# Decode attention with conditioned layer norms: one section of w_mod loaded later, in eight transfers of eight partitions

## The chip, the core and the metric

One core of a Trainium2 chip runs the whole program. It has TensorE (PE, with its weight loads listed apart as PEld), VectorE (DVE), ScalarE (ACT), GpSimd (POOL) and SyncE (SP), which here only issues transfers, and 16 DMA engines that move data from HBM into the 128 partitions of SBUF. The metric is the device time of one execution in microseconds.

## What is computed

One token is decoded for each of 4 batch rows. x and c are 4 x 512; the K and V caches have 32 heads, 4096 positions and 128 numbers a head, in bf16, 128 MB each. Everything else is small beside them.

```python
    x = A_x
    mod = (_silu(c) @ w_mod).reshape(c.shape[0], 6, 1, -1)
    sa, ca, ga, sb, cb, gb = (mod[:, 0].copy(), mod[:, 1].copy(), mod[:, 2].copy(), mod[:, 3].copy(), mod[:, 4].copy(), mod[:, 5].copy())
    h = _layernorm(x, axis=-1) * (1 + ca) + sa
    x = x + ga * _A_ref(h, A_k_cache, A_v_cache, A_wq, A_wo)
    h = _layernorm(x, axis=-1) * (1 + cb) + sb
    x = x + gb * _B_ref(h, B_w_in, B_w_sp, B_b_sp, B_w_out)
    return x
```

_A_ref is softmax attention over the caches with wq before it and wo behind it. _B_ref is a gated MLP: gelu(x @ w_in) is split in two halves of 896, the second is normalised and gates the first, and w_out brings it back to 512. w_mod is 512 x 3072, so each of its six sections (sa, ca, ga, sb, cb, gb) is 512 x 512, 0.5 MB.

## The kernel before

The caches are cut into 32 tiles (NT) of 4 heads of one batch row. A tile of K, and one of V, is 4 MB: each partition gets 32 KB that lie together in HBM. Iteration i of the main loop works on tile i in stages that are spread over iterations: `mult` (L288, DVE) multiplies K by the query in two halves, `reduce_d` (L294, PE) sums over the 128 numbers with an identity matmul, `sum8` and `scores` (L303 to L326, DVE and ACT) make the maximum and the exponentials of tile i - 1, `pv` (L366, PE) multiplies tile i - 2 by V, and `o_pick`, `o_cols` and `o_scale` (L374 to L408) finish tile i - 3.

The order of all instructions is written out by hand, and each engine takes its own in that order. All large loads are issued by SP, one queue, in program order: wq_sb (L89), wm_sb (L92), K of tiles 0 and 1 and V of tile 0 (L104), and then, in iteration i, K of tile i + 2 and V of tile i. K tiles have two buffers named "kt", V tiles two named "vt". A K load waits until both `mult` and `reduce_d` of the buffer's old tile are done; a V load waits for `pv` of its old tile. A wait of SP holds up every transfer behind it.

What the change touches:

- wm_sb (L90 to L92) holds the first five sections of w_mod: row p*4 + j lies in partition p. `mod_cols` (L236 to L245) multiplies chosen sections by cT, the transposed silu(c): sections 0 and 1 ahead of the loop (L254), sections 2, 3 and 4 in iteration 2 (L571 to L573), whose result is modT. Section 5 is loaded at the end into a "vt" buffer (wg_sb, L600 to L602) and used at L715.
- c (c_sb) and x (x_sb) are loaded by ACT (L83, L85), four rows each. `rows_to_cols` (L184) transposes them on PE; the silu runs on the transposed c, 128 x 16 (L224 to L234).
- cbT, the part of modT for section 4, gets 1 added in iteration 5 (L593). It is used at L645 and L658.
- After iteration 2 the pool with wq_sb and wm_sb is given back, and the pool wts takes its place: wo_sb, wo_last, win_sb and wout_sb.
- In iteration 30 the last loads are queued: V of tile 31 in five pieces into a "kt" buffer, win_sb (L597), wout_sb (L599), wg_sb (L602).
- Behind the loop the last tiles are finished, and then come the MLP's matmuls, `gate` (L684) on win_sb, L707 on wout_sb, L715 on wg_sb, and the output (L753).

Of the kernel before, what the change touches and what calls it, by code (L numbers as in the profile page):

```python
# [8 lines left out]
BF16 = mybir.dt.bfloat16  # L9
F32 = mybir.dt.float32  # L10
AF = mybir.ActivationFunctionType
ALU = mybir.AluOpType
# [12 lines left out]
def kernel(  # L25
# [16 lines left out]
    nc = tc.nc  # L42
    P = 128
    B, _, D = A_x.shape
    _, H, SK, DH = A_k_cache.shape
    F = B_w_in.shape[1]
    FH = F // 2
    DJ = D // P
    NF = F // P
    NH = FH // P  # L50
    NJ = SK * HQ // P
# [13 lines left out]
    consts = ctx.enter_context(tc.tile_pool(name="consts", bufs=1))  # L65
    kvp = ctx.enter_context(tc.tile_pool(name="kv", bufs=2))
# [6 lines left out]
    def ps_sm(shape, dtype=F32):  # L73
        return psum.tile(shape, dtype, name="sm", bufs=3)
# [6 lines left out]
    pre = pre_cm.__enter__()  # L81
    c_sb = pre.tile([B, D], BF16, name="c_sb")
# [4 lines left out]

    wq_sb = pre.tile([P, DJ, H * DH], BF16, name="wq_sb")
    nc.sync.dma_start(out=wq_sb, in_=A_wq.rearrange("(p j) n -> p j n", p=P))  # L89
    wm_sb = pre.tile([P, DJ, 5 * D], BF16, name="wm_sb")  # L90
    wm = w_mod.rearrange("(p j) n -> p j n", p=P)
    nc.sync.dma_start(out=wm_sb, in_=wm[:, :, 0:5 * D])  # L92

    def kv_view(cache, i):
        g, b = divmod(i, B)
# [16 lines left out]
    def load_v(i):  # L112
# [8 lines left out]
    ident_bf = consts.tile([P, P], BF16, name="ident_bf")  # L121
# [13 lines left out]

    st2 = consts.tile([P, 2, DJ + 1], F32, name="st2")
    nc.vector.memset(st2, 0.0)
    nc.vector.memset(st2[:, 1, DJ:], LN_EPS * D / P)

# [3 lines left out]
        out=sel32, in_=ident_f.rearrange("p (q r) -> p r q", r=R), axis=AX.X, op=ALU.add  # L143
# [10 lines left out]
    for g in range(G):  # L154
        nc.vector.tensor_reduce(out=selg[:, g:g + 1], in_=idr[:, g], axis=AX.XY, op=ALU.add)
    nc.vector.tensor_reduce(
        out=sel4, in_=ident_f.rearrange("p (c b) -> p b c", b=B), axis=AX.X, op=ALU.add
# [3 lines left out]
        out=mask8, in_=ident_f.rearrange("p (h u) -> p h u", h=2 * HQ), axis=AX.X, op=ALU.add  # L161
# [3 lines left out]
    x1w = consts.tile([P, DJ, R], F32, name="x1w")  # L165
    nc.gpsimd.memset(x1w, 0.0)
    cT = consts.tile([P, DJ, B], BF16, name="cT")

    consts.tile([P, 512], mybir.dt.uint8, name="gap")
    wk.tile([P, 32], mybir.dt.uint8, name="gap", bufs=1)  # L170
    pbds, opss = [], []
    for k in range(3):
        t = consts.tile([P, NJ, HQ], BF16, name=f"pbd{k}")
        nc.gpsimd.memset(t, 0.0)
        pbds.append(t)
    for k in range(2):
        t = psum.tile([P, G, DH], F32, name=f"ops{k}", bufs=1)
# [3 lines left out]
    def bc(ap, n):  # L181
        return ap[:, None, :].to_broadcast([P, n, ap.shape[-1]])

    def rows_to_cols(src):  # L184
        t = ps_sm([P, DJ, B], BF16)
        for j in range(DJ):
            nc.tensor.transpose(t[:, j, :], src[0:B, j:D:DJ], ident_bf[0:B, 0:B])
        return t

    def across(rhs, mat):  # L190
# [13 lines left out]
    def normed(pool, src, name, then=None, last=None):  # L204
# [16 lines left out]
        rsqrt(rs, v, 1.0, eps)  # L221
        return xc, rs

    cps = rows_to_cols(c_sb)  # L224
    cx = pre.tile([P, DJ, B], F32, name="cx")
    nc.vector.tensor_copy(out=cx, in_=cps)
    sg = pre.tile([P, DJ, B], F32, name="sg")
    nc.vector.tensor_scalar(
        out=sg, in0=cx, scalar1=-60.0, scalar2=-1.0, op0=ALU.max, op1=ALU.mult
    )  # L230
    nc.scalar.activation(out=sg, in_=sg, func=AF.Exp)
    nc.vector.tensor_scalar_add(out=sg, in0=sg, scalar1=1.0)
    nc.vector.reciprocal(out=sg, in_=sg)
    nc.vector.tensor_tensor(out=cT, in0=cx, in1=sg, op=ALU.mult)  # L234

    def mod_cols(s0, n, dst):  # L236

        for m in range(n):
            s, j = divmod(m, DJ)
            c0 = (s0 + s) * D + j  # L240
            for k in range(DJ):
                nc.tensor.matmul(  # L242
                    dst[:, m, :], lhsT=wm_sb[:, k, c0:c0 + (P - 1) * DJ + 1:DJ], rhs=cT[:, k, :],
                    start=(k == 0), stop=(k == DJ - 1),
                )  # L245
# [11 lines left out]
        out=hs, in0=modA[:, DJ:2 * DJ, :], scalar=1.0, in1=xn, op0=ALU.add, op1=ALU.mult  # L257
# [174 lines left out]
    for n in set(SETS):  # L432
        picks[n] = consts.tile([P, n, P], BF16, name=f"pick{n}")
        for a in range(n):
            u = P // n
            nc.vector.tensor_copy(
                out=picks[n][:, :, a * u:(a + 1) * u],
                in_=ident_bf.rearrange("p (u r) -> p r u", r=n),
# [77 lines left out]
        nc.vector.tensor_tensor(out=a, in0=a, in1=wp, op=ALU.add)  # L516

    modT = consts.tile([P, 3 * DJ, B], F32, name="modT")

    g8 = consts.tile([P, 2, B], F32, name="g8")  # L520
    sp_t = consts.tile([1, 2], BF16, name="sp_t")
# [8 lines left out]
    for i in range(NT):  # L530
        more = list(QPLAN.get(i, ()))
        mult(i, 0)
        if i >= 1:
            scores(i - 1)
        if i >= 2:
            norm_b(i - 2)
        add_up()
        rows_up()
        dealt()
        if i >= 3:  # L540
            o_pick(i - 3)
        reduce_d(i, 0)
        if i >= 3:
            o_cols(i - 3)
        if more:
            queries(more.pop(0))
        mult(i, 1)
        if i >= 1:
            norm_r(i - 1)
        if i >= 3:  # L550
            o_scale(i - 3)
        sum8(i, 0)
        reduce_d(i, 1)
        load_k(i + 2)
        if i >= 1:
            norm_a(i - 1)
        project()
        if i - 3 in ends:
            deal(ends[i - 3])
        while more:  # L560
            queries(more.pop(0))
        if i >= 2:
            pv(i - 2)
        if i == 0:
            load_v(1)
        elif 2 <= i < L:
            load_v(i)
        if i == 2:
            nc.scalar.dma_start(out=sp_t[:, 0:1], in_=B_w_sp[0:1, 0:1])
            nc.scalar.dma_start(out=sp_t[:, 1:2], in_=B_b_sp.rearrange("(a b) -> a b", b=1))  # L570
            mps = ps_sm([P, 3 * DJ, B])  # L571
            mod_cols(2, 3 * DJ, mps)
            nc.vector.tensor_copy(out=modT, in_=mps)  # L573
            pre_cm.__exit__(None, None, None)
            wts = tl = ctx.enter_context(tc.tile_pool(name="wts", bufs=1))
            wo_sb = wts.tile([P, H - HQ, D], BF16, name="wo_sb")
            wo_last = wts.tile([P, HQ, D], BF16, name="wo_last")
            hl = (H - HQ) * DH
            h0 = 0
            for n in SETS:  # L580
                nc.sync.dma_start(
                    out=wo_sb[:, h0:h0 + n, :],
                    in_=A_wo[h0 * DH:(h0 + n) * DH].rearrange("(p r) n -> p r n", p=P),
                )
                h0 += n
            nc.sync.dma_start(out=wo_last, in_=A_wo[hl:H * DH].rearrange("(q p) n -> p q n", p=P))
        if i == 5:
            sps = ps_sm([P, 2])
            nc.tensor.matmul(sps, lhsT=ones_b, rhs=sp_t, start=True, stop=True)
            nc.vector.tensor_copy(out=spf, in_=sps)  # L590
            nc.vector.tensor_copy(out=g8[:, 1, :], in_=spf[:, 0:1].to_broadcast([P, B]))
            cbT = modT[:, 2 * DJ:3 * DJ, :]
            nc.vector.tensor_scalar_add(out=cbT, in0=cbT, scalar1=1.0)  # L593
        if i == L - 1:
            load_v(L)
            win_sb = wts.tile([P, DJ, F], BF16, name="win_sb")
            nc.sync.dma_start(out=win_sb, in_=B_w_in.rearrange("(p j) n -> p j n", p=P))  # L597
            wout_sb = wts.tile([P, NH, D], BF16, name="wout_sb")
            nc.sync.dma_start(out=wout_sb, in_=B_w_out.rearrange("(j p) n -> p j n", p=P))  # L599
            wg_sb = kvp.tile([P, NJ, DH], BF16, name="vt", bufs=2)  # L600
            wg_sb = wg_sb.rearrange("p n d -> p (n d)")[:, 0:DJ * D].rearrange("p (k n) -> p k n", k=DJ)
            nc.sync.dma_start(out=wg_sb, in_=wm[:, :, 5 * D:])  # L602

    gaT = modT[:, 0:DJ, :]
# [24 lines left out]
    def sums():  # L629
# [21 lines left out]
        out=nv2, in0=mq2[:, 0:1], scalar=mq2[:, 0:1], in1=mq2[:, 1:2],  # L651
        op0=ALU.mult, op1=ALU.subtract,
# [6 lines left out]
        out=hl, in0=xs, scalar=mq2[:, 0:1], in1=cbT[:, :, BL], op0=ALU.subtract, op1=ALU.mult  # L659
    )  # L660
    nc.vector.scalar_tensor_tensor(
        out=hT2[:, :, BL], in0=hl, scalar=rsl, in1=sbT[:, :, BL], op0=ALU.mult, op1=ALU.add
# [4 lines left out]
        out=x1m, in0=x1[:, :, :, None].to_broadcast([P, DJ, B, HQ]),  # L667
        in1=mask4[:, None, None, :].to_broadcast([P, DJ, B, HQ]), op=ALU.mult,
    )
    x1r = ps_sm([B * DJ, P])  # L670
    for k in range(DJ):
        nc.tensor.matmul(
            x1r[:, k:P:DJ], lhsT=x1m[:, k].rearrange("p b j -> p (b j)"), rhs=sel32,
            start=True, stop=True,
# [4 lines left out]
    def gate(h):  # L679
# [21 lines left out]
        out=zz.rearrange("p f g b -> p g b f"), in0=z1[:, None].to_broadcast([P, 2, B, NH]),  # L701
        in1=st3[:, 0:2], op=ALU.mult,
    )
    y = ps_q()[:, 0:DJ * 2 * B].rearrange("p (j g b) -> p j g b", j=DJ, g=2)
    for j in range(DJ):
        for f in range(NH):
            nc.tensor.matmul(  # L707
                y[:, j], lhsT=wout_sb[:, f, j * P:(j + 1) * P], rhs=zz[:, f],
                start=(f == 0), stop=(f == NH - 1),
# [3 lines left out]
    for j in range(DJ):  # L713
        for k in range(DJ):
            nc.tensor.matmul(  # L715
                gb[:, j, :], lhsT=wg_sb[:, k, j * P:(j + 1) * P], rhs=cT[:, k, :],
                start=(k == 0), stop=(k == DJ - 1),
# [3 lines left out]
        out=mq3, in_=ps3.rearrange("p (g b f) -> p g b f", g=2, b=B), axis=AX.X, op=ALU.add  # L721
# [4 lines left out]
        out=rs3, in0=mq3[:, 1], scalar=LN_EPS, in1=rs3, op0=ALU.add, op1=ALU.subtract  # L726
# [3 lines left out]
        out=g8[:, 0, :], in0=mq3[:, 0, :], scalar=-1.0, in1=g8[:, 1, :], op0=ALU.mult, op1=ALU.mult  # L730
# [5 lines left out]
        out=t3[:, 2], in0=yb[:, 0], scalar1=spf[:, 1:2], scalar2=None, op0=ALU.mult  # L736
    )
    nc.vector.tensor_tensor(
        out=g8, in0=g8, in1=rs3[:, None, :].to_broadcast([P, 2, B]), op=ALU.mult
    )  # L740
    nc.vector.tensor_tensor(
        out=t3[:, 0:2], in0=g8[:, :, :, None].to_broadcast([P, 2, B, DJ]), in1=yb, op=ALU.mult
# [3 lines left out]
        out=tt, in_=t3.rearrange("p g b j -> p b j g"), axis=AX.X, op=ALU.add  # L746
# [37 lines left out]
```

## Time and profile before

| what | value |
|---|---|
| time, median of 3 runs | 667.87 us (667.51 to 667.99) |
| span of the profiled execution | 665.8 us |
| bytes read from HBM | 282.73 MB, 425 GB/s over the span |
| PE, DVE, ACT busy | 60%, 63%, 13% |
| DMA share of 16 engines, 20 to 620 us | 1.00, at 432 GB/s |
| a K load, from issue to landing (31 of them) | 23.0 us, median |
| a V load, from issue to landing (31 of them) | 30.7 us, median |
| granted TensorE clock, mean | 0.828 |

The span is from the first instruction to the last on the profiled core; the runs' times include what lies around it, some 2 us. Slices and groups of the page are means over the whole execution; the end of the kernel is read from the chain of waits and the timeline. A queue "instruction" in the DMA table moves the program itself, not data. The trace also lists each DMA packet with its start, length, size and queue; it does not name the engine.

### The profile page before, as it was taken

Reading aid. Unit: us, or ns where it says so; the run is one execution under the profiler, and the core shown is the slowest. Engines: PE = TensorE matmul, PEld = TensorE weight load, DVE = VectorE, ACT = ScalarE, POOL = GpSimd, SP = SyncE. Lnnn points to the kernel's source line nnn. Section 1 sums busy time; section 2 is a strip of 40 time slices with the busy share of each in tenths; the row PEclk is TensorE's granted clock in tenths of the full one; section 3 lists DMA queues with packets and bytes.
Section 4 is the critical chain, followed back from the end, with each engine's and each line's share of the span. In section 5 each row is a group of like instructions: output and inputs, shape, how many; then the busy total and the mean of one; then the engine's idle time right before and its main releaser. Section 6 shows DMA issues by size and latency. Waiting matters only on the chain.

```text
span 665.8 us, 6509 instructions
## 1 busy us (share of the span) xinstructions
PE 399.3 (60%) x2674; PEld 175.4 (26%) x2674; DVE 419.5 (63%) x589; ACT 85.0 (13%) x278; POOL 3.8 (1%) x17
## 2 busy tenths in 40 slices
PE   1195795556556746754665467566555468666675
PEld 0132331222222312222222222222222223322245
DVE  3485592776565777655567756657765566776833
ACT  1021120111011111101111110111111011111112
POOL 1000000000000000000000000000000000000000
PEclk9998987777898778789877778787777897887975
DMA  8999999999999999999999999999999999999996
GB/s 363 452 419 433 431 417 435 436 437 422 439 432 438 422 439 433 436 423 436 435 431 426 438 435 432 426 436 437 431 426 437 435 429 432 433 436 421 438 419 234
DMA packets 13377, 283.15 MB, mean 425 GB/s; under 512 B 1308, under 2 KB 3236, under 8 KB 4132
## 3 DMA queue, kind: packets, MB, share of 16 engines
q1 hardware_dynamic: 13328, 282.73, 98.9%
q8 instruction: 21, 0.34, 0.2%
q14 instruction: 8, 0.07, 0.0%
q10 hardware_dynamic: 20, 0.01, 0.0%
HBM read 282.73 MB, written 0.00 MB: 425 GB/s over the span
## 4 chain that ended last, share of the span: by engine, by line
DMA 56%; DVE 28%; PE 13%; issue 1%; SPq 1%; ACT 0%; DVEq 0%
DMA kt<-in_A_k_cache_dram 52%; DVE kt L288 21%; PE red L294 11%; DMA win_sb<-in_B_w_in_dram 5%; DVE osb L378 2%; DVE S L303 1%; DVE mrow L312 1%; DVE osb L374 1%; PE ops L366 1%; SPq L104 1%; DVE mt L316 1%; DVE nM L318 0%; PE qps L274 0%; DVE mb L314 0%; DVE nM L319 0%
## 5 line engine op out<-in xcount | busy, mean ns | idle before, releaser
L294 PE MATMUL red<-kt,ident_bf 128*128 128x512 bf16 x1024 | 301.5, 461 | 236.4 <-DVE kt L288 236.4
L288 DVE TENSOR_TENSOR kt<-kt,qbc 128x8192 bf16<-128x8192 bf16 x64 | 282.8, 4420 | 185.2 <-DMA kt<-in_A_k_cache_dram 184.2
L294 PEld LDWEIGHTS <-ident_bf 128*128 128x128 bf16 x1024 | 118.9, 116 | 411.5 <-issue 285.8
L326 ACT ACTIVATE pbd<-S,nM 32x128 bf16<-32x128 f32 x128 | 73.8, 577 | 505.3 <-DVE nM L319 463.2
L366 PE MATMUL ops<-vt,pbd 128*16 128x512 bf16 x992 | 62.6, 388 | 1.4 <-DMA vt<-in_A_v_cache_dram 1.4
L303 DVE TENSOR_REDUCE S<-red 128x64 f32<-128x512 f32 x64 | 43.8, 684 | 5.8 <-PE red L294 5.8
L378 DVE SCALAR_TENSOR_TENSOR osb<-ops,selg,osb 128x128 f32<-128x128 f32 x93 | 32.6, 351 | 3.3
L326 ACT ACTIVATION_READ_ACCUMULATOR pbd<-S,nM 32x1 f32 x128 | 32.0, 250 | 0.0
L366 PEld LDWEIGHTS <-pbd 128*16 128x16 bf16 x992 | 23.2, 90 | 30.7 <-issue 8.5
L386 PEld LDWEIGHTS sm<-sel,osb 128*128 128x128 f32 x62 | 11.7, 194 | 7.4 <-issue 2.2
L374 DVE TENSOR_SCALAR osb<-ops,selg 128x128 f32<-128x128 f32 x31 | 10.1, 325 | 5.3 <-PE ops L366 5.3
L386 PE MATMUL sm<-sel,osb 128*128 128x4 f32 x62 | 9.2, 219 | 2.1 <-DVE osb L378 2.0
L278 ACT CAST qbc<-qps 128x512 bf16<-128x512 f32 x8 | 4.7, 585 | 45.3 <-PE qps L274 45.3
L274 PE MATMUL qps<-wq_sb,hTb 128*32 128x512 bf16 x128 | 9.2, 412 | 1.6 <-DVE hTb L262 0.9
L312 DVE TENSOR_REDUCE mrow<-S 128x1 f32<-128x128 f32 x32 | 9.2, 286 | 1.1
L242 PE MATMUL sm<-cT,wm_sb 128*128 128x4 bf16 x80 | 3.0, 173 | 8.3 <-DMA wm_sb<-in_w_mod_dram 8.3
L316 DVE STREAM_TRANSPOSE mt<-mb 128x32 f32<-128x32 f32 x32 | 6.8, 212 | 1.1
L337 DVE TENSOR_SCALAR rsb<-mask,rs 128x4 f32<-128x4 f32 x32 | 7.2, 224 | 0.4 <-ACT pbd L326 0.4
L318 DVE TENSOR_REDUCE nM<-mt 128x1 f32<-128x32 f32 x32 | 6.0, 186 | 1.1
L314 DVE COPY mb<-mrow 128x32 f32<-128x32 f32 x32 | 5.8, 181 | 1.1
L491 PE MATMUL sm<-wo_sb,od 128*4 128x512 bf16 x24 | 5.7, 379 | 0.0
L319 DVE TENSOR_SCALAR nM<-nM 128x1 f32<-128x1 f32 x32 | 4.9, 153 | 1.1
(136 smaller groups left out, 88.8 us busy)
## 6 DMA issues: line engine op xcount, KB each, us to landing
kt<-in_A_k_cache_dram SPq DMA_DIRECT2D x31, 4096.0 KB, 23.0
vt<-in_A_v_cache_dram SPq DMA_DIRECT2D x31, 4096.0 KB, 30.7
wq_sb<-in_A_wq_dram SPq DMA_DIRECT2D x1, 4096.0 KB, 12.3
kt<-in_A_k_cache_dram SPq DMA_DIRECT2D x2, 2048.0 KB, 16.7
wo_sb<-in_A_wo_dram SPq DMA_DIRECT2D x3, 1024.0 KB, 22.9
kt<-in_A_v_cache_dram SPq DMA_DIRECT2D x3, 1024.0 KB, 25.5
wm_sb<-in_w_mod_dram SPq DMA_DIRECT2D x1, 2560.0 KB
win_sb<-in_B_w_in_dram SPq DMA_DIRECT2D x1, 1792.0 KB
```

The costliest lines, as they stand in the source:

```text
L274: nc.tensor.matmul(qp[R * q:R * (q + 1)], lhsT=hTb[:, k, b, :], rhs=wq_v[:, k, gs, q, :], start=(k == 0), stop=(k == DJ - 1), tile_positio ...
L288: nc.vector.tensor_tensor(out=kt, in0=kt, in1=bc(qbc[:, g, b, :], KC), op=ALU.mult)
L294: nc.tensor.matmul(red, lhsT=ident_bf, rhs=kt[:, :, m * RD:(m + 1) * RD], start=(m == 0), stop=(m == DH // RD - 1),)
L303: nc.vector.tensor_reduce(out=st[i, "S"][:, kc * KC:(kc + 1) * KC], in_=st.pop((i, "red", kc)), axis=AX.X, op=ALU.add,)
L312: nc.vector.tensor_reduce(out=mrow, in_=S, axis=AX.X, op=ALU.max)
L316: nc.vector.transpose(mt, mb)
L326: nc.scalar.activation(out=pbd[r, :, q], in_=S[r, :], func=AF.Exp, bias=nM[r, :], scale=att_scale, accum_out=rs[r, :],)
L337: nc.vector.tensor_scalar(out=st[g, "rsb"][:, b, :], in0=mask4, scalar1=st.pop((i, "rs")), scalar2=None, op0=ALU.mult)
L366: nc.tensor.matmul(opss[i % 2][g:g + G * HQ], lhsT=pbds[i % 3][:, n, :], rhs=vts[i][:, n, :], start=(m < 4), stop=(m >= NJ // G - 4), tile ...
L374: nc.vector.tensor_scalar(out=osb, in0=ops[:, 0, :], scalar1=selg[:, 0:1], scalar2=None, op0=ALU.mult)
L378: nc.vector.scalar_tensor_tensor(out=osb, in0=ops[:, g, :], scalar=selg[:, g:g + 1], in1=osb, op0=ALU.mult, op1=ALU.add,)
L386: nc.tensor.matmul(op, lhsT=st.pop((i, "osb")), rhs=sel4, start=True, stop=True)
```

## The change

Section 4 of w_mod no longer comes with wm_sb. It gets a tile of its own, w8, on 64 partitions with 8 rows each, filled by eight transfers of 64 KB, one per iteration from 3 to 10, each into eight partitions that lie four apart (0 to 31 in the first four, 32 to 63 in the others). Its product is formed in iteration 14 by 32 matmuls over 64 rows, and 1 is added as the result is taken out of PSUM. For that the silu is taken on the 4 x 512 rows before they are transposed, and transposed twice: into cT (128 x 16) and into cT8 (64 x 32). w_out loses its own tile: it and the gate weights share one "vt" buffer, so that w_out's load now waits for the buffer as well.

```diff
-    wm_sb = pre.tile([P, DJ, 5 * D], BF16, name="wm_sb")
+    wm_sb = pre.tile([P, DJ, 4 * D], BF16, name="wm_sb")
     wm = w_mod.rearrange("(p j) n -> p j n", p=P)
-    nc.sync.dma_start(out=wm_sb, in_=wm[:, :, 0:5 * D])
+    nc.sync.dma_start(out=wm_sb, in_=wm[:, :, 0:4 * D])
...
-    def rows_to_cols(src):
-        t = ps_sm([P, DJ, B], BF16)
-        for j in range(DJ):
-            nc.tensor.transpose(t[:, j, :], src[0:B, j:D:DJ], ident_bf[0:B, 0:B])
+    def rows_to_cols(src, n=DJ):
+        t = ps_sm([D // n, n, B], BF16)
+        for j in range(n):
+            nc.tensor.transpose(t[:, j, :], src[0:B, j:D:n], ident_bf[0:B, 0:B])
         return t
...
-    cps = rows_to_cols(c_sb)
-    cx = pre.tile([P, DJ, B], F32, name="cx")
-    nc.vector.tensor_copy(out=cx, in_=cps)
-    sg = pre.tile([P, DJ, B], F32, name="sg")
+    sg = pre.tile([B, D], F32, name="sg")
     nc.vector.tensor_scalar(
-        out=sg, in0=cx, scalar1=-60.0, scalar2=-1.0, op0=ALU.max, op1=ALU.mult
+        out=sg, in0=c_sb, scalar1=-60.0, scalar2=-1.0, op0=ALU.max, op1=ALU.mult
     )
     nc.scalar.activation(out=sg, in_=sg, func=AF.Exp)
     nc.vector.tensor_scalar_add(out=sg, in0=sg, scalar1=1.0)
     nc.vector.reciprocal(out=sg, in_=sg)
-    nc.vector.tensor_tensor(out=cT, in0=cx, in1=sg, op=ALU.mult)
+    cs = pre.tile([B, D], BF16, name="cs")
+    nc.vector.tensor_tensor(out=cs, in0=c_sb, in1=sg, op=ALU.mult)
+    nc.vector.tensor_copy(out=cT, in_=rows_to_cols(cs))
+    nc.vector.tensor_copy(out=cT8, in_=rows_to_cols(cs, K8))
...
-            mps = ps_sm([P, 3 * DJ, B])
-            mod_cols(2, 3 * DJ, mps)
-            nc.vector.tensor_copy(out=modT, in_=mps)
+            mps = ps_sm([P, 2 * DJ, B])
+            mod_cols(2, 2 * DJ, mps)
+            nc.vector.tensor_copy(out=modT[:, 0:2 * DJ], in_=mps)
...
+            w8 = wts.tile([P2, K8, D], BF16, name="w8")
+            w8v = w_mod[:, 4 * D:5 * D].rearrange("(h e s j) n -> h s e j n", h=2, e=8, s=4)
+        if 3 <= i < 11:
+            h, r = divmod(i - 3, 4)
+            nc.sync.dma_start(out=w8[32 * h + r:32 * h + 32:4], in_=w8v[h, r])
...
-            cbT = modT[:, 2 * DJ:3 * DJ, :]
-            nc.vector.tensor_scalar_add(out=cbT, in0=cbT, scalar1=1.0)
+        if i == 14:
+            mp8 = ps_sm([P, DJ, B])
+            for j in range(DJ):
+                for k in range(K8):
+                    nc.tensor.matmul(
+                        mp8[:, j, :], lhsT=w8[:, k, j:D:DJ], rhs=cT8[:, k, :],
+                        start=(k == 0), stop=(k == K8 - 1),
+                    )
+            nc.vector.tensor_scalar_add(out=cbT, in0=mp8, scalar1=1.0)
...
-            wout_sb = wts.tile([P, NH, D], BF16, name="wout_sb")
+            ends_sb = kvp.tile([P, NJ, DH], BF16, name="vt", bufs=2).rearrange("p n d -> p (n d)")
+            wout_sb = ends_sb[:, 0:NH * D].rearrange("p (f n) -> p f n", f=NH)
             nc.sync.dma_start(out=wout_sb, in_=B_w_out.rearrange("(j p) n -> p j n", p=P))
-            wg_sb = kvp.tile([P, NJ, DH], BF16, name="vt", bufs=2)
-            wg_sb = wg_sb.rearrange("p n d -> p (n d)")[:, 0:DJ * D].rearrange("p (k n) -> p k n", k=DJ)
+            wg_sb = ends_sb[:, NH * D:(NH + DJ) * D].rearrange("p (k n) -> p k n", k=DJ)
             nc.sync.dma_start(out=wg_sb, in_=wm[:, :, 5 * D:])
```

More of the change, by code (lines that the diff above doesn't have):

```diff
@@ L48 @@
     DJ = D // P
+    P2 = P // 2
+    K8 = D // P2
     NF = F // P
@@ L167 @@
     cT = consts.tile([P, DJ, B], BF16, name="cT")
+    cT8 = consts.tile([P2, K8, B], BF16, name="cT8")
     consts.tile([P, 512], mybir.dt.uint8, name="gap")
@@ L518 @@
     modT = consts.tile([P, 3 * DJ, B], F32, name="modT")
+    cbT = modT[:, 2 * DJ:3 * DJ, :]
     g8 = consts.tile([P, 2, B], F32, name="g8")
```

## Prediction

> **What bounds the kernel now.** I read the page first (DMA row, queues, chain), then the chain in order of time, the timeline of the end, and last the trace's records of single DMA packets.
>
> ```profile
> DMA  8999999999999999999999999999999999999996
> q1 hardware_dynamic: 13328, 282.73, 98.9%
> q8 instruction: 21, 0.34, 0.2%
> q14 instruction: 8, 0.07, 0.0%
> DMA 56%; DVE 28%; PE 13%; issue 1%; SPq 1%; ACT 0%; DVEq 0%
> kt<-in_A_k_cache_dram SPq DMA_DIRECT2D x31, 4096.0 KB, 23.0
> ```
>
> The 16 DMA engines are never idle between the first and the last microseconds. The chain passes through DVE and PE only because a K load needs a free buffer; such a load then takes 23.0 us to land, though its 8 packets per engine last 9.7 us. So about 13 us of other transfers lie ahead of it, and a compute step that is a few microseconds late costs nothing. Bytes per DMA engine set the time. The end of the chain:
>
> ```profile
> 625.92 31.81 DMA win_sb<-in_B_w_in_dram
> 657.73 0.05 issue
> 657.78 1.67 PE red L684 x56
> ```
>
> and the timeline there:
>
> ```profile
> 656.88 0.23 DVE L661 SCALAR_TENSOR_TENSOR hT<-hl,rsl,modT 128x4 bf16<-128x4 f32 x1 [0.37 <-ACT rsl L202]
> 657.78 1.65 PE L684 MATMUL red<-hT,win_sb 128*128 128x4 bf16 x56 [0.78 <-DMA win_sb<-in_B_w_in_dram]
> 660.15 0.89 PE L707 MATMUL qps<-zz,wout_sb 128*128 128x8 bf16 x28 [0.20 <-DVE zz L700]
> 661.38 0.58 PE L715 MATMUL sm<-cT,vt 128*128 128x4 bf16 x16 [0.34 <-DMA vt<-in_w_mod_dram]
> ```
>
> PE is ready 0.65 us before win_sb has landed, and wout_sb and the gate weights land just as they are wanted. The last three landings set the end, and a landing is that of the slowest engine.
>
> **Which engine is slowest.** The trace has start, length and size of every packet. In the stream a packet starts 3 to 4 ns before the one ahead on its engine ends, so packets chain into 16 lanes; their sizes (8 of 32 KB and a 4-byte one per K or V load) confirm it. All lanes run at 1.21 us per 32 KB, yet they finish win_sb up to 4.64 us apart. The steps all come where an instruction block (q8, q14 above) is fetched in a lane: 16 KB delays it by about 1.42 us, 8 KB by 0.84. Us behind the earliest lane at win_sb, my letters:
>
> ```
> lanes with the 16 KB blocks: 2.78 2.80 4.33 4.24 4.64 4.17 3.93 3.54
> lane V, with most of the 8 KB blocks: 4.21
> the other seven: 0.50 0.03 1.34 0.00 0.07 1.18 0.79
> ```
>
> **The change, by parts.** *wm_sb smaller.* Its 32 packets per lane of 5 KB take 6.18 us. The last pieces of V (8 packets of 4 KB in 1.25 us) give 32 x 0.156 = 4.99. Every lane gains 1.2 us.
>
> *The eight transfers.* 64 rows of 1 KB each. In the trace x_sb (4 partitions) uses 4 lanes, sp_t (1 partition) one, which is among those 4, and out (16 rows) 16. So 8 partitions use 8 lanes, very likely a set that holds the 4. The third of those 4 is V or a lane 1 ns beside it at that moment which gets 16 KB blocks; both are 4.2 us late at the end. Each of the eight lanes gets 8 x 8 = 64 packets. wo_last and the gate weights, with the same 1 KB rows, take 1.36 us for 32: 42.5 ns each, so 2.72 us. Bounds: 37.8 ns by the share of a 32 KB packet (2.42 us); 46 ns, as x_sb's packets lasted, with 0.06 us per transfer for its semaphore packet and a longer first packet (359 for 309 ns after some wo_sb transfers): 3.4 us. I take 2.72, since those rows have the same source rows. The eight lanes lose 2.72 - 1.2 = 1.52 us (1.2 to 2.2); the other eight gain 1.2.
>
> [...] No row here shows a gap between queued transfers: the 8 KB packets of wo_sb run through four transfers at 2.45 us each, 8 x 306 ns.
>
> *End.* V was 4.21, becomes 4.21 + 1.52 = 5.73 on the old scale; the latest of the others falls to 4.64 - 1.2 = 3.44. The latest landing moves from 4.64 to 5.73: +1.09 us. V's last 8 KB block falls into win_sb's packets; VectorE's stream is one instruction longer by then, so it stays there. hT2 is later too, by less: at the last piece of V lane V stands at 3.38 + 1.52 = 4.90 against 4.33, +0.57, and hT2 had 0.65 to spare plus win_sb's own +1.09. wout_sb and the gate weights shift by the same 1.09.
>
> *SP's queue.* Eight issues of about 0.35 us each, behind the V load of iterations 3 to 10. Behind them stands the next K load, which waits 13 to 14 us for L288 anyhow: nothing; without that cover 0.35 us each. w_out now waits for pv(29), whose matmuls end at 639.1, and is issued there rather than at 633.5; the gate weights behind it went out only at 649.5. The stream ahead lasts past 655 us: nothing. Without that cover 5.6 us.
>
> *Iteration 2 and 14.* At iteration 2 16 of 48 matmuls go: 16/48 of this row, -0.59 us, on a stretch followed by a K load with 27.5 us to landing: nothing.
>
> ```profile
> 76.63 1.76 PE L242 MATMUL sm<-cT,wm_sb 128*128 128x4 bf16 x48
> 308.38 1.90 PE L366 MATMUL ops<-vt,pbd 128*16 128x512 bf16 x32
> 312.64 4.42 DVE L288 TENSOR_TENSOR kt<-kt,qbc 128x8192 bf16<-128x8192 bf16 x1 [6.84 <-DMA kt<-in_A_k_cache_dram]
> ```
>
> At iteration 14 there are 32 new ones of 64 rows: 32 x 36.7 ns = 1.2 us (at most 32 x (0.173 + 0.118) = 9.3 if nothing overlaps). They run after pv(12), end at 308.38 + 1.90 + 1.2 = 311.5, and the add on DVE, ahead of the next L288, waits for them to 311.7. That L288 waits for K until 312.64: nothing. At 9.3 us it would start 7.2 late, inside the 13 us of queue.
>
> *Prologue.* The silu now runs on 4 x 512 instead of 128 x 16. Three DVE passes at 0.43 to 0.6 (128x512 copies and memsets), an exponential 0.58 (the 512-wide cast), a reciprocal by the 0.25 us of 16 columns against 0.17 of 4: 6.7 ns a column, 3.6 us. With 8 more transposes (0.58) and a copy, cT is there near 11.6 instead of 5.9, and xn, 3.4 us behind it, near 15.
>
> ```profile
> 11.73 0.17 DVE L252 TENSOR_TENSOR xn<-xc_ln,rs_ln 128x16 f32<-128x16 f32 x1 [0.60 <-ACT rs_ln L202]
> 19.23 1.23 PE L242 MATMUL sm<-cT,wm_sb 128*128 128x4 bf16 x32 [8.31 <-DMA wm_sb<-in_w_mod_dram]
> 28.96 4.43 DVE L288 TENSOR_TENSOR kt<-kt,qbc 128x8192 bf16<-128x8192 bf16 x1 [5.62 <-DMA kt<-in_A_k_cache_dram]
> ```
>
> wm_sb lands at about 18.0 now, K at 27.8: 3 us of cover, 5.6 more behind. Nothing; without it the 3.4 us or so would shift the first L288. K, and with it the whole early chain, comes 1.2 us sooner, as does the stream, so the one near-empty moment of the queue (two lanes idle 0.2 and 0.55 us before K of iteration 4) stays as it is.
>
> **Sum.** Against the profiled execution's span of 665.8: 665.8 + 1.09 = 666.9. The runs' median is 667.87, 2.07 above that span: 668.96, say 669.0. Own range 668.7 to 669.7 (lane cost 1.2 to 2.2).
>
> **Rivals.** *Spread over all lanes.* Then each lane gets 32 packets, +1.36 - 1.2 = +0.16: 668.0. For it: all big loads do so. Against: x_sb and sp_t. [...] Chance 0.10.
>
> *The eight lanes miss the late ones.* Then the late lanes gain 1.2, the eight stay below (1.34 + 1.52 = 2.86 against 3.44), and the time falls to 666.7: faster. For it: seven lanes have over 3 us in hand, and the 16 KB blocks keep to eight lanes. Against: x_sb's third lane is late on either reading. It decides if V is outside. Chance 0.08.
>
> *Late lanes with 16 KB blocks among the eight.* 4.64 + 1.52 = 6.16: +1.52, 669.4, slower. For it: which four complete the eight no row shows. Against: at least three of x_sb's four lanes are early ones. Chance 0.15.
>
> *Each small transfer opens a gap in its lanes.* The first packets of the kernel took 1.22 to 2.26 us rather than 1.21, some 0.7 too much; eight times that is 5.6: 674.5. From 0.1 us each it decides. Against: the gapless wo_sb. Chance 0.07.
>
> **How the numbers follow.** The forecast has 0.60. 0.2% is 1.34 us, about what a measurement of this kernel tells from no change: the bounds are 666.5 and 669.2. The forecast lies inside, with a third of its range above. Slower: 0.20 + 0.15 + 0.07 = 0.42. Faster: about half of the second rival, with noise 0.05. Within: 0.53. The range 667.5 to 670.3 holds the forecast, the first rival and the third, 0.85, and leaves out 666.7 and 674.5.
>
> **What would show it.** In the packets of the changed kernel: 8 lanes with 64 packets of 1 KB more, lane V some 2.3 us behind all others at the end, win_sb landing 1.1 us later than 657.7, the gaps before L684, L707 and L715 as now. L288 of iteration 15 still waiting for DMA. xn before wm_sb. Wrong if the latest lane at win_sb is none of the eight, if a lane stands idle behind a 1 KB packet, or if L684 no longer waits for win_sb.

## The result and the profile after

The change made the kernel slower: 672.37 us (median of 6 runs, 672.31 to 672.56) against 667.87 for the kernel before on the same chip (5 runs, 667.37 to 668.54), a ratio of 1.0069 with an interval of 1.0057 to 1.008, or +4.50 us. Three runs that a disturbance lengthened (694.74 and 685.02 us of the kernel before, 680.40 of aligned_16 below) are left out of the medians and ratios of this text. The forecast was 669.0, with a range up to 670.3; the time lies outside it. The span of the profiled execution went from 665.8 to 670.4 us, +4.6.

From the page of the changed kernel: the DMA row of the 40 slices, the line that sums up the packets, the queues (packets, MB, share of 16 engines) and the engines' shares of the chain.

```profile
DMA  8999999999999999999999999999999999999995
...
DMA packets 13953, 283.15 MB, mean 422 GB/s; under 512 B 1372, under 2 KB 3812, under 8 KB 4708
...
q1 hardware_dynamic: 13904, 282.73, 98.7%
q8 instruction: 21, 0.34, 0.2%
...
DMA 60%; DVE 29%; PE 10%; issue 1%; SPq 0%; ACT 0%; DVEq 0%
```

The kernel is bound by the DMA engines as before: they are never idle, and they move the same 282.73 MB. What fell is the mean rate, from 425 to 422 GB/s. The number of packets tells more. The same line of the kernel before is this:

```profile
DMA packets 13377, 283.15 MB, mean 425 GB/s; under 512 B 1308, under 2 KB 3236, under 8 KB 4132
```

There are 64 more packets under 512 bytes (in the kernel before, 80 transfers on q1 left 1280 packets of 4 bytes, 16 each, one in each lane; so the 64 of the eight transfers, eight each, put these on eight engines), and 576 more under 2 KB: these 64 and 512 rows of 1 KB. So the change made the transfers that the prediction counted. The timeline of the end of the changed kernel (start, duration, instruction, and in brackets the idle time before it with what ended it):

```profile
661.68 0.23 DVE L678 SCALAR_TENSOR_TENSOR hT<-hl,rsl,modT 128x4 bf16<-128x4 f32 x1 [0.36 <-ACT rsl L205]
662.26 1.65 PE L701 MATMUL red<-hT,win_sb 128*128 128x4 bf16 x56 [0.55 <-DMA win_sb<-in_B_w_in_dram]
664.77 0.91 PE L724 MATMUL qps<-zz,vt 128*128 128x8 bf16 x28 [0.34 <-DMA vt<-in_B_w_out_dram]
666.17 0.59 PE L732 MATMUL sm<-cT,vt 128*128 128x4 bf16 x16 [0.49 <-DMA vt<-in_w_mod_dram]
```

The lines L701, L724 and L732 are L684, L707 and L715 of the kernel before. L701 and L732 still wait for their transfers, and L724, whose last wait was for DVE before, now waits for its transfer too; the gaps are 0.55, 0.34 and 0.49 us, and were 0.78, 0.20 and 0.34. L701 starts 4.48 us later than its 657.78 of before, and the whole span is 4.6 us longer. So no more than some 0.1 us was lost behind the stream: the stream itself is longer. It did not lengthen in the iterations with the small transfers alone. Two stretches of the changed kernel, and the same of the kernel before (stretch, length, busy time and count of PE, PEld, DVE, ACT, POOL, then the granted clock, the DMA share and GB/s):

```profile
77.00:300.00 223.00, 126.17 (x750) 53.27 (x751) 144.35 (x177) 25.43 (x88) 0.00 (x0) 0.82 1.00 429
300.00:620.00 320.00, 198.88 (x1156) 84.47 (x1155) 209.91 (x268) 39.34 (x136) 0.00 (x0) 0.82 1.00 431
```

```profile
77.00:300.00 223.00, 133.06 (x798) 56.18 (x797) 146.70 (x187) 26.29 (x91) 0.00 (x0) 0.80 1.00 431
300.00:620.00 320.00, 196.75 (x1135) 83.68 (x1133) 210.50 (x264) 38.50 (x134) 0.00 (x0) 0.83 1.00 432
```

Engines at a share of 1.00 move fewer bytes per second, also from 300 us on, where no small transfer is left. The rates are rounded, so the single packets were read. Mean duration on queue q1, in ns:

```
packet        before   after    per engine (count before / 16)
32 KB         1216.3   1220.3   504
8 KB           309.8    313.6    48
1 KB            46.0     48.4   120
16 KB instruction block (q8)    949.7   1086.9   1.3
```

Before, nearly every 32 KB packet takes 1213 ns (7957 of 8064 do); after, most take 1214 to 1222, and so they do from the first K loads on, ahead of any small transfer. One 4 MB load follows another in 9.714 instead of 9.683 us. Over some 65 such loads that makes 2.0 us, which no term of the prediction holds.

What had moved was found in the addresses that the compiled program gives the tiles inside a partition. The new cT8 (64 bytes per partition) stands in the pool `consts`, ahead of all other pools:

```
tile              before            after
kt (two buffers)  35840, 68608      35904, 68672
wm_sb             206336            206400
win_sb            204288            212544
```

Before, every large tile starts at a multiple of 512 bytes; after, 64 bytes past one. This became the theory: a transfer into a misaligned tile costs a little more per packet. Its rival was the prediction's, that the small transfers cost more than counted.

### The profile page after: what moved, and what is told of

Same layout as the page of the kernel before. It is cut to its first block, busy times and chain, and to the rows that moved or that the text cites. A ratio compares the mean times of both kernels' runs of the same rounds, so it can differ in the third digit from the quotient of the medians.

```text
span 670.4 us, 6568 instructions
## 1 busy us (share of the span) xinstructions
PE 398.8 (59%) x2698; PEld 176.3 (26%) x2698; DVE 423.9 (63%) x590; ACT 85.4 (13%) x278; POOL 3.7 (1%) x17
## 3 DMA queue, kind: packets, MB, share of 16 engines
q1 hardware_dynamic: 13904, 282.73, 98.7%
HBM read 282.73 MB, written 0.00 MB: 422 GB/s over the span
## 4 chain that ended last, share of the span: by engine, by line
DMA 60%; DVE 29%; PE 10%; issue 1%; SPq 0%; ACT 0%; DVEq 0%
DMA kt<-in_A_k_cache_dram 54%; DVE kt L291 22%; PE red L297 9%; DMA vt<-in_A_v_cache_dram 3%; DMA vt<-in_w_mod_dram 3%; DVE osb L381 2%; DVE S L306 2%; DVE mrow L315 1%; DVE osb L377 1%; DVE mt L319 1%; DVE nM L321 0%; DVE mb L317 0%; DVE nM L322 0%; PE ops L369 0%; DVE qbc L513 0%
## 5 line engine op out<-in xcount | busy, mean ns | idle before, releaser
L291 DVE TENSOR_TENSOR kt<-kt,qbc 128x8192 bf16<-128x8192 bf16 x64 | 282.8, 4420 | 186.4 <-DMA kt<-in_A_k_cache_dram 185.4
```

Of the source, the lines that this page charges most:

```text
L291: nc.vector.tensor_tensor(out=kt, in0=kt, in1=bc(qbc[:, g, b, :], KC), op=ALU.mult)
```

## The experiments

There were nine, in three groups; kernels of a group are compared with runs of the kernel before of that group (medians 667.65, 667.91 and 667.85 us).

**The shift taken out of the changed kernel (after_aligned).** The filler tile beside cT8 is made 64 bytes smaller, so that what follows stands where it stood before.

```diff
-    consts.tile([P, 512], mybir.dt.uint8, name="gap")
+    consts.tile([P, 448], mybir.dt.uint8, name="gap")
```

> The changed kernel with the filler tile 'gap' cut from 512 to 448 bytes a partition, so that every large DMA destination starts at a multiple of 512 bytes again, as before the change (the 64 bytes of cT8 had moved them all by 64). Address theory: 32 KB packets go back from 1215 to 1213 ns and the period of a 4 MB load from 9.714 to 9.683 us; over some 65 loads' worth of bytes that is 2.0 us, and with the cheaper instruction blocks and 1 KB packets 2.5 to 3: 669.4 to 669.9, which leaves the lane cost of the prediction (+1.1 to +1.9 on 667.9). Rival, lanes alone (the eight transfers cost far more than thought, the slower packets are the chip's): 672.4 as before.

668.83 us (11 runs, 668.6 to 669.85), ratio 1.0018 [1.0009, 1.0027]. The rival's 672.4 is ruled out. Above the kernel before of its own group the kernel is now 668.83 - 667.65 = 1.18 us, so this edit alone takes back 4.50 - 1.18 = 3.3 us. That is somewhat more than the 2.5 to 3 us that the address theory gave, and the time lies below its 669.4 to 669.9. The end of the timeline:

```profile
657.64 0.23 DVE L678 SCALAR_TENSOR_TENSOR hT<-hl,rsl,modT 128x4 bf16<-128x4 f32 x1 [0.37 <-ACT rsl L205]
659.15 1.65 PE L701 MATMUL red<-hT,win_sb 128*128 128x4 bf16 x56 [1.39 <-DMA win_sb<-in_B_w_in_dram]
```

L701 waits 1.39 us for win_sb now and starts 1.37 later than L684 did before. The mean 32 KB packet is back at 1216.2 ns.

**The shift alone (before_off64).** The kernel before, with its filler 64 bytes larger.

```diff
-    consts.tile([P, 512], mybir.dt.uint8, name="gap")
+    consts.tile([P, 576], mybir.dt.uint8, name="gap")
```

> The kernel before with the filler tile grown from 512 to 576 bytes and nothing else: all large destinations start 64 bytes past a multiple of 512. Address theory: the packets of the changed kernel (1215 and 1222 ns for 32 KB), 9.71 us a load, 670.4 to 670.9. Rival, lanes alone: 667.9 unchanged.

670.53 us (5 runs, 670.43 to 670.71), ratio 1.0041 [1.0029, 1.0053]: +2.88 us for an edit that adds no instruction and no byte moved. Where it goes can be read from two starts of L288, the first of the kernel and one near the end, both of which wait for K. The kernel before, then this one:

```profile
618.97 4.43 DVE L288 TENSOR_TENSOR kt<-kt,qbc 128x8192 bf16<-128x8192 bf16 x1 [1.46 <-DMA kt<-in_A_k_cache_dram]
```

```profile
29.18 8.76 DVE L288 TENSOR_TENSOR kt<-kt,qbc 128x8192 bf16<-128x8192 bf16 x2 [5.63 <-DMA kt<-in_A_k_cache_dram]
...
621.40 4.42 DVE L288 TENSOR_TENSOR kt<-kt,qbc 128x8192 bf16<-128x8192 bf16 x1 [1.58 <-DMA kt<-in_A_k_cache_dram]
```

Before, the first was at 28.96 us (the prediction's block shows it), so it is 590.01 from one to the other, and 592.22 here: 2.21 us more over the same loads. By packets (their mean excess over before in ns, times the count per engine): 504 x 3.5 + 120 x 3.0 + 48 x 4.4 = 2.3 us; the three 16 KB instruction blocks that the latest lane gets, 0.1 us dearer each, add some 0.3.

**How far off, and where the boundary is (before_off32, before_off128, before_off256).** The same edit with 544, 640 and 768 bytes.

> The kernel before with the filler tile 32 bytes larger: large destinations 32 bytes past a multiple of 512. Address theory with a boundary of 64 bytes or more: as before_off64, 670.5, or worse. If only the multiple of 32 counts: 667.7.

> The kernel before with the filler tile 128 bytes larger: large destinations 128 bytes past a multiple of 512. If the boundary that counts is 128 bytes or less: 667.7. If it is 256 or 512: about 670.5.

> The kernel before with the filler tile 256 bytes larger: large destinations 256 bytes past a multiple of 512. If the boundary that counts is 256 bytes: 667.7. If it is 512: about 670.4, as 32, 64 and 128 bytes gave.

```
filler     shift   us, median (range, runs)           ratio [95%]                  mean 32 KB packet, ns
before     0       667.85 (last group)                1                            1216.3
544        32      671.33 (671.02 to 671.40, 4)       1.0051 [1.0035, 1.0066]      1220.8
576        64      670.53 (670.43 to 670.71, 5)       1.0041 [1.0029, 1.0053]      1219.8
640        128     670.38 (670.35 to 670.49, 4)       1.0036 [1.0023, 1.0050]      1219.6
768        256     667.46 (667.24 to 668.10, 10)      0.9994 [0.9985, 1.0004]      1216.0
```

The shift by 256 bytes is free (ratio 0.9994), those by 32, 64 and 128 are not (1.0051, 1.0041 and 1.0036), and the smaller ones cost no less. So the size of the shift isn't it: in these five kernels the dearer packets (1219.6 to 1220.8 ns against 1216.0 and 1216.3) go with large tiles that start off a multiple of 256 bytes. Shifts between 128 and 256 were not tried. Why it costs what it costs, no run shows. The late L288 of the free one stands where it stood before (618.97):

```profile
618.92 4.42 DVE L288 TENSOR_TENSOR kt<-kt,qbc 128x8192 bf16<-128x8192 bf16 x1 [1.46 <-DMA kt<-in_A_k_cache_dram]
```

**The rest of the change without the small transfers (aligned_none).** The filler of 448, and w8 filled with zeros in place of the eight transfers: section 4 of w_mod is not loaded.

```diff
-        if 3 <= i < 11:
-            h, r = divmod(i - 3, 4)
-            nc.sync.dma_start(out=w8[32 * h + r:32 * h + 32:4], in_=w8v[h, r])
+        if i == 3:
+            nc.gpsimd.memset(w8, 0.0)
```

> As after_aligned, but the eight transfers are left out and w8 is filled with zeros by GpSimd, so section 4 of w_mod does not enter the result. Lane theory: every lane is 1.2 us shorter than before the change: 666.7 (666.4 to 667.0). If something other than the transfers makes the changed kernel slow (prologue, iteration 14, the wait of w_out), it stays above 667.5.

666.58 us (11 runs, 666.03 to 668.5), ratio 0.9986 [0.9977, 0.9995], -1.07 us. That is wm_sb's smaller load (1.2 us per lane) and nothing else: the silu on four partitions, the matmuls of iteration 14 and the late issue of w_out are all in this kernel and cost nothing that can be measured. The eight transfers cost 668.83 - 666.58 = 2.25 us on the path; by the prediction's lanes it was 1.09 + 1.2 = 2.29. Its L701 line, to be set beside 659.15 above:

```profile
656.93 1.66 PE L700 MATMUL red<-hT,win_sb 128*128 128x4 bf16 x56 [1.18 <-DMA win_sb<-in_B_w_in_dram]
```

**The same bytes over all lanes (even_four).** As after_aligned, but w8 on 128 partitions with 4 rows each, four transfers of 128 KB, and cT instead of cT8.

```diff
-            w8 = wts.tile([P2, K8, D], BF16, name="w8")
+            w8 = wts.tile([P, DJ, D], BF16, name="w8")
+            w8v = w_mod[:, 4 * D:5 * D].rearrange("(p j) n -> p j n", p=P)
+        if i in (3, 5, 7, 9):
+            j = (i - 3) // 2
+            nc.sync.dma_start(out=w8[:, j, :], in_=w8v[:, j, :])
```

> As after_aligned, but w8 lies on all 128 partitions and comes in four transfers of 128 KB (one row of 1 KB per partition, iterations 3, 5, 7, 9), so every lane writes its usual partitions and gets 4 x 8 packets of 1 KB; the product uses cT. Lane theory: each lane gets 1.36 us instead of 2.72 on eight of them: aligned_none's 666.6 + 1.36 = 667.9, as before the change, and some 0.9 below after_aligned. Rival, a small transfer as such costs every lane (the 0.44 us that each of aligned_16's eight cost): 668.4 or more.

667.4 us (11 runs, 667.16 to 669.38), ratio 1.0000 [0.9991, 1.0009]. The lane count gives +0.16 for it, and no difference is measured. So what the eight transfers cost in after_aligned comes from loading eight of sixteen lanes, and not from the section being loaded late. The number of transfers differs too, four here and eight there; but in after_aligned each delays its lanes by 0.345 us, which is what its eight packets of 43 ns take, and that leaves no cost for a transfer as such.

```profile
657.66 1.65 PE L701 MATMUL red<-hT,win_sb 128*128 128x4 bf16 x56 [0.45 <-DMA win_sb<-in_B_w_in_dram]
```

**The same transfers over 16 engines (aligned_16).** Meant as the first rival's case: as after_aligned, but eight transfers of 16 partitions, eight apart.

```diff
-            nc.sync.dma_start(out=w8[32 * h + r:32 * h + 32:4], in_=w8v[h, r])
+            nc.sync.dma_start(out=w8[r:P:8], in_=w8v[r])
```

(with w8 on 128 partitions, r = i - 3, and w8v = "(e s j) n -> s e j n" with e=16, s=8)

> As after_aligned, but w8 lies on 128 partitions and each of the eight transfers fills sixteen partitions that lie eight apart, four rows each; its product uses cT. Same bytes, same iterations. Lane theory: sixteen lanes with 32 packets of 1 KB each instead of eight with 64, so every lane gets 1.36 us and loses 1.2 of wm_sb: 668.1 (667.7 to 668.4), 1.3 us or more below after_aligned. Rival, what costs is a small transfer as such: the same as after_aligned.

This missed. 672.59 us (5 runs, which scatter: 670.19 to 674.29), ratio 1.0072 [1.0055, 1.0088], where 668.1 was expected. The profile is that of the fastest run, at 670.19; what the others lost beyond that is in no trace. Its packet line, its first stretch, and the same stretch of after_aligned:

```profile
DMA packets 14017, 283.15 MB, mean 424 GB/s; under 512 B 1436, under 2 KB 3876, under 8 KB 4772
```

```profile
77.00:300.00 223.00, 126.82 (x750) 53.21 (x750) 143.80 (x177) 25.47 (x88) 0.00 (x0) 0.82 1.00 427
```

```profile
77.00:300.00 223.00, 129.63 (x754) 54.19 (x755) 145.57 (x183) 25.45 (x88) 0.00 (x0) 0.81 1.01 432
```

All 16 engines were used (128 semaphore packets more than in the kernel before, 16 for each transfer), but the rate in the stretch of the small transfers fell to 427 GB/s, against 432 in after_aligned. In the packets each transfer delays the mean lane by some 0.4 us (two loads with it mostly take 19.7 to 19.9 us, where two loads alone take 19.36), against 0.17 for its four packets in a lane. So which partitions an engine writes seemed to matter, and the next kernel tries that.

**The same eight engines, other partitions (consecutive).** Eight transfers as in the change, each into eight partitions that lie side by side.

```diff
-            nc.sync.dma_start(out=w8[32 * h + r:32 * h + 32:4], in_=w8v[h, r])
+            nc.sync.dma_start(out=w8[8 * t:8 * t + 8], in_=w8v[t])
```

(with t = i - 3, w8v = "(t e j) n -> t e j n", and the filler of 448)

> As after_aligned, but each of the eight transfers fills eight partitions that lie side by side (0 to 7, 8 to 15, ...) instead of four apart. Same lanes, packets and iterations. Crossing theory (aligned_16 was slow because its lanes wrote partitions that other lanes write in the large loads): slower than after_aligned, by the 0.27 us per transfer beyond its packets that aligned_16 showed or more, 671 to 675, with uneven times. Rival, the partitions do not matter, only the lanes: 668.8.

674.47 us (5 runs, 673.32 to 676.22), ratio 1.0100 [1.0083, 1.0117]: 6.56 us above the kernel before, where after_aligned is 1.18 above it, with the same packets and eight engines for each transfer as there.

```profile
77.00:300.00 223.00, 124.08 (x749) 52.54 (x750) 139.85 (x177) 25.46 (x88) 0.00 (x0) 0.83 1.00 423
300.00:620.00 320.00, 197.18 (x1150) 83.43 (x1151) 212.70 (x269) 39.34 (x136) 0.00 (x0) 0.81 1.00 432
```

The loss is in the first stretch, 423 GB/s against 432, and over once the transfers are. Two loads with a transfer between them take 19.7 to 20.3 us, some 0.7 us more than two alone for the mean lane, and single 1 KB packets last up to 226 ns instead of 46. The median lies in the 671 to 675 that the crossing theory gave: with eight engines for each transfer, the kernel takes 674.47 us with partitions side by side and 668.83 with partitions four apart. What in the placement costs this, no run shows. The rows of w_mod that a transfer reads change along with the partitions: consecutive reads 64 neighbouring rows, the change eight pieces of 8 rows that start 32 rows apart. Whether the reading side has a part in the cost was not tried.

## Why the prediction was wrong

**What failed.** The sentence "All lanes run at 1.21 us per 32 KB" was read from the kernel before and carried over to the kernel after, and every term of the sum rested on it. The prediction does not speak of the tiles' addresses. They were part of the change, through cT8's 64 bytes, and the missing term is 2.88 us (before_off64) to 3.3 us (after_aligned). The two agree in sign and size but not exactly: 1.18 for the lanes, as measured in after_aligned, and 2.88 make 4.06 of the 4.50. The other 0.4 is within what the intervals allow. The packets put it on the latest lanes: in the changed kernel the last two finish win_sb 7.80 and 7.93 us behind the earliest, in after_aligned 5.54 and 7.01. Dearer instruction blocks there would be of that size (three at 1.55 instead of 1.42 us); it isn't settled.

**What held.** With the addresses put right the kernel takes 668.83 us, where 669.0 was forecast, and the steps can be held against it:

- *Eight lanes, 64 packets each.* Right. In after_aligned each of the eight transfers delays eight lanes by 0.345 us, 2.76 in all; 2.72 was worked out. No gap opened behind them, so the fourth rival fell.
- *The latest lane.* Right in that it was lane V, the one with the 8 KB instruction blocks, and one of the eight. Us behind the earliest lane at win_sb, in after_aligned:

```
the eight lanes with w8:  3.21 2.53 4.24 2.60 2.56 7.01 (V) 5.45 5.54
the others:               3.95 2.72 4.20 3.96 3.27 3.38 1.14 0.00
```

  V is some 1.5 us behind the next, not 2.3, since two lanes with 16 KB blocks are among the eight as well. The prediction's third rival had it right that late lanes with 16 KB blocks are among the eight, but they don't decide. L701, which waits for win_sb, starts 1.37 us later than L684 did, where 1.09 was predicted, and the median is 1.18 up.
- *wm_sb smaller.* 1.2 us per lane predicted, 1.07 measured with aligned_none.
- *The first rival, spread over all lanes.* As a picture of this change it was wrong (eight lanes). As a sum it was about right, if the spread is over 128 partitions: +0.16, and even_four shows no difference.
- *What was costed at nothing.* aligned_none holds all of it, and it costs nothing. The predicted times of the prologue can also be read, in the changed kernel:

```profile
6.17 3.34 DVE L233 RECIPROCAL sg<-sg 4x512 f32<-4x512 f32 x1
10.60 0.17 DVE L236 COPY cT<-sm 128x16 bf16<-128x16 bf16 x1 [0.38 <-PE sm L190]
15.15 0.18 DVE L255 TENSOR_TENSOR xn<-xc_ln,rs_ln 128x16 f32<-128x16 f32 x1 [0.60 <-ACT rs_ln L205]
18.20 1.23 PE L245 MATMUL sm<-cT,wm_sb 128*128 128x4 bf16 x32 [3.87 <-DMA wm_sb<-in_w_mod_dram]
27.97 8.76 DVE L291 TENSOR_TENSOR kt<-kt,qbc 128x8192 bf16<-128x8192 bf16 x2 [5.64 <-DMA kt<-in_A_k_cache_dram]
```

  The reciprocal on 4 x 512 takes 3.34 us (3.6 predicted), cT is there at 10.8 (11.6), xn at 15.3 (15), and L245 still waits 3.87 us for wm_sb, so the longer silu is hidden. The first L291 waits 5.64 us for K, as before.
- *Iteration 14.* Right:

```profile
310.77 1.90 PE L369 MATMUL ops<-vt,pbd 128*16 128x512 bf16 x32
312.61 1.22 PE L606 MATMUL sm<-cT,w 64*128 64x4 bf16 x32
...
315.91 4.43 DVE L291 TENSOR_TENSOR kt<-kt,qbc 128x8192 bf16<-128x8192 bf16 x1 [1.87 <-DMA kt<-in_A_k_cache_dram]
```

  The 32 matmuls take 1.22 us (1.2 predicted). DVE's idle time before this L291 is 1.87 us instead of 6.84, since DVE first waits for them with the add; then it still waits for K, so nothing is lost.

**The range.** It left out everything above 670.3. Its upper end holds the forecast with its dearest lane cost (669.7) and the third rival (669.4); that every packet on all lanes could get dearer was not among the rivals. A range from rows of the kernel before can't hold such a term, and a change of the memory map should have been one: a shift of every tile that lies behind the new one can be read from the diff (a new tile in `consts`, no change to the filler) without a run.

## What to carry to other kernels

When DMA bytes set the time, look at the addresses as well as the byte counts: one small tile added in front of the large ones made the mean 32 KB packet of this kernel 0.3% dearer (1220.3 ns for 1216.3), and 64 bytes less in a filler tile put it right (1216.2). Account for the stream by single DMA engines: in after_aligned the lanes finish win_sb up to 7.01 us apart, and the matmuls behind it wait for the latest. There eight transfers that use half of the engines, with the latest among them, cost the end 2.25 us (against aligned_none), where an even share of their packets is 1.36 by the prediction's estimate; the same bytes over 128 partitions (even_four) left the kernel at the time of the kernel before (ratio 1.0000). Small transfers into few partitions slowed the large ones beside them in two of the placements tried (some 0.4 and 0.7 us each in aligned_16 and consecutive), so measure the placement and not only the size.

## What was not expected of the hardware

- In the kernel before, whose large tiles start at multiples of 512 bytes, nearly every 32 KB packet takes 1213 ns (7957 of 8064); in the changed kernel, where they start 64 bytes past one, most take 1214 to 1222. The means are 1216.3 and 1220.3 ns, and 1216.0 with the shift of 256 bytes (before_off256). The 16 KB instruction blocks in the same lanes go from a mean of 950 to one of 1087 ns.
- In this full queue, eight engines that write 64 KB into eight neighbouring partitions hold up the mean of the sixteen lanes by some 0.7 us (consecutive), sixteen engines into partitions eight apart by some 0.4 (aligned_16), and eight into partitions four apart only their own lanes, by 0.345 (after_aligned).
- Not tried: small transfers on the early lanes only. It could gain little: what there is to gain is wm_sb's smaller load, 1.2 us per lane, and aligned_none, which has that and no small transfer at all, is 1.07 us faster. None of the kernels that do all of the work was measurably faster than the kernel before.
